# A planner that knows an engine's wait for its own result, finer steps, layer 1 in jobs of 256 tokens, and early room for layer 2's first weights

## The chip, the cores and the metric

The program runs on one core of one Trainium2 chip. The metric is device time in microseconds (us) of one execution, as the median of several. TensorE is called PE here, VectorE DVE, ScalarE ACT, GpSimd POOL, and SyncE, which issues the DMAs, SP.

## What is computed

Three parts run one after the other, all in fp32:

```python
# attention with a complex decay, 4 batches x 8 heads x 768 steps x 48
S_re, S_im = ar*S_re - ai*S_im + k[t] (x) v[t],  ar*S_im + ai*S_re
y[t] = q[t] . S_re                       # 3072 tokens of 384 after the heads are joined
# layer 1, 384 -> 2048 -> 384
x = (relu(x @ w_in) ** 2) @ w_out
# layer 2, the same sizes
h = x @ w2_in;  out = (h * sigmoid(1.702 * h)) @ w2_out
```

## The kernel before

The attention is cut into 12 **units** of 256 tokens, each in two **chunks** of 128. `normalize` scales a unit's decays; `scan` forms their running products: seven steps within groups of 8 (one product L405, then the two planes L408 and L409), five doubling steps across groups (L426 to L429), the exclusive products (L437, L438, into `eexc`) and their use (L448 to L452). It then multiplies q into `tq` (L463) and k into `tk` (L505). Both go through DRAM and come back as `qs`, from which `chunk` computes on PE the scores `pa` (L571), the transposed keys `pk` (L589), the output `px` (L604 to L621), the state `pt` (L641) and its rotation `zs` (L656). Nearly all of the scan is DVE work.

The layers run as **jobs** of tokens (L28). Layer 1 (l=0) has three jobs of 256 tokens, then six of 384; layer 2 (l=1) has eight of 384. A job has 16 **steps** m, one for each 128 of the 2048 inner columns: a first product `h` (L753), ACT's and DVE's work on it (L758 to L768), and a second product into three accumulators (L798, L800). Job 0 multiplies in fp32. From job 1 (first product) and job 3 (second product) on, each fp32 product is made of three with rounded parts (high x high, low x high, high x low), 18 matmuls a step. The rounding of `g` to `gh` is ACT's (L767) and the remainder `gl` DVE's (L768): one `gl` for every step of such a job.

The weights arrive as raw 64-bit words and are decoded by ACT and DVE (L683 to L691, `wf`) and split into a high and a low part (L698, L699). There are 32 such pieces a layer, two a step. All of them live in one ring `w` of 66 buffers, so a piece of layer 2 gets a buffer when one of layer 1 is given back.

The order on all engines is written by a planner (`Plan`, L64) that is run while the program is built. It keeps a list of operations with costs and due times and simulates the engines: it takes the operation that can start first, on a tie the most urgent. What one engine hands to another costs a latency (L69). An operation that needs a result of its own engine could start at once in the plan (L178). What the planner calls one operation stays together: `fin` is two instructions, one doubling step is four (L431). Engines work strictly in the order so made; the waits between them are real semaphores.

Three lines that set the shape of the work:

```python
JOBS = [(0, 256)] * 3 + [(0, 384)] * 6 + [(1, 384)] * 8
...
x.ready = max(x.ready, o.end if x.eng != o.eng else t + o.ns)
...
o = buf("o" if l == 0 else "nt", [128, MX], name="o")
```

Of the kernel before, what the change touches and what calls it, by code (L numbers as in the profile page):

```python
# [24 lines left out]
J = 8  # L25
U = 32 * J
MX = 384
JOBS = [(0, 256)] * 3 + [(0, 384)] * 6 + [(1, 384)] * 8  # L28
NAT1 = 1
# [30 lines left out]
class Op:  # L60
    __slots__ = ("eng", "ns", "lat", "fn", "due", "prio", "pred", "succ", "bufs", "wait", "start", "end", "idx", "ready")


class Plan:  # L64
# [17 lines left out]
    def op(self, eng, ns, fn, r=(), w=(), lat=None, due=1e12):  # L82
        o = Op()
        o.eng, o.ns, o.fn, o.due = eng, float(ns), fn, due
        o.lat = self.LAT[eng] if lat is None else lat
        o.idx, o.succ, o.start = len(self.ops), [], None
        pred = set()
        for k in r:
            if k in self.lastw:
                pred.add(self.lastw[k])  # L90
        for k in w:
# [12 lines left out]
        for x in o.bufs:  # L104
            x.left += 1
        self.ops.append(o)
        return o

    def run(self, issue=None):
# [33 lines left out]
        while len(order) < len(ops):  # L143
# [53 lines left out]
def fast(ctx: ExitStack, tc: tile.TileContext, q, k, v, a_re, a_im, w1, w2, out, flag):  # L197
# [87 lines left out]
    def setup():  # L285
        def consts():
            P.memset(tiny, 2.0 ** -56)
            P.memset(shb, SH * math.log(2.0))
            P.memset(eexc, 0.0)
            P.memset(eexc[:, 0, :, 0:1], 1.0)  # L290

        def more():
            for t in vt + st:
                P.memset(t, 0.0)
            make_identity(nc, ident[:, 0:R])
            P.tensor_copy(ident[:, R:R + D], ident[:, 0:D])
# [4 lines left out]
        op("POOL", 800, consts, w=["consts", "eexc"])  # L301
        op("POOL", 3500, more, w=["v0", "v1", "st0", "st1", "ident", "ones", "tops"], due=30e3)
# [91 lines left out]
    def scan(u):  # L394
# [4 lines left out]
        for j in range(1, J):  # L399
# [6 lines left out]

            def fin(j=j, m=m):
                V.tensor_tensor(ab()[:, 0, j], m()[:, 0, 0], m()[:, 1, 1], ALU.subtract)  # L408
                V.tensor_tensor(ab()[:, 1, j], m()[:, 0, 1], m()[:, 1, 0], ALU.add)  # L409

            js = slice(j, j + 1)
            op("DVE", ve(384), go, r=planes(ab, slice(j - 1, j + 1)), w=[m])
            op("DVE", 2 * ve(96), fin, r=[m], w=planes(ab, js))

        lastp = planes(ab, slice(J - 1, J))
        h = 1
        while h < 32:
            m = buf("mm", [128, 2, 2, 48], name="mm")

            def go(h=h, m=m):  # L420
# [3 lines left out]
                t1, t2 = (m()[:, c].rearrange("p c (n s) -> p c n s", s=h) for c in range(2))  # L424
                lr, li = (gv[:, c, :, 0, h - 1:h].unsqueeze(1).to_broadcast([128, 2, nb, h]) for c in range(2))
                V.tensor_tensor(t1, sec, lr, ALU.mult)  # L426
                V.tensor_tensor(t2, sec, li, ALU.mult)
                V.tensor_tensor(sec[:, 0], t1[:, 0], t2[:, 1], ALU.subtract)
                V.tensor_tensor(sec[:, 1], t1[:, 1], t2[:, 0], ALU.add)  # L429

            op("DVE", 2 * ve(96) + 2 * ve(48), go, r=lastp, w=lastp + [m])  # L431
            h *= 2


        def groups():
            g = ab()[:, :, J - 1].rearrange("p c (x r) -> p c x r", r=32)
            V.tensor_copy(eexc[:, 0:2, :, 1:32], g[:, :, :, 0:31])  # L437
            V.tensor_scalar(eexc[:, 2, :, 1:32], g[:, 1, :, 0:31], -1.0, None, ALU.mult)  # L438

        op("DVE", 310, groups, r=lastp, w=["eexc"])  # L440
        ee = eexc.rearrange("p c x r -> p c (x r)")
        for js in (slice(0, HJ), slice(HJ, J - 1)):
# [6 lines left out]

            op("DVE", ve(192 * n), lambda p2=p2, n=n, mul=mul: mul(p2()[:, :, :n], 1), r=["eexc", *planes(ab, js)], w=[p2])  # L450
            op("DVE", ve(192 * n), lambda js=js, mul=mul: mul(ab()[:, :, js], 0), r=["eexc", *planes(ab, js)], w=planes(ab, js))
# [103 lines left out]
    def chunk(i, due):  # L555
# [115 lines left out]
    def decode(l, m, g):  # L671
# [19 lines left out]
        op("DVE", ve(384), lambda: V.tensor_tensor(w32(), w32(), words()[1], ALU.add), r=[w_, raw, (raw, 0)], w=[w_])  # L691

    def split(l, m, g):

        w_ = wf[l, m, g]
        high = wh[l, m, g] = buf("w", [128, DM], F32R, name="wh")
        low = wl[l, m, g] = buf("w", [128, DM], F32R, name="wl")
        op("ACT", ac(384), lambda: A.copy(high(), w_()), r=[w_], w=[high])  # L698
        op("DVE", ve(384), lambda: V.tensor_tensor(low(), w_(), high().bitcast(F32), ALU.subtract), r=[w_, high], w=[low])  # L699

# [36 lines left out]
    def first_product(j, m, due):  # L737
# [34 lines left out]
    def second_product(j, m, parts, due):  # L772
# [84 lines left out]
    for j, (l, t0, n) in enumerate(jobs):  # L857
# [215 lines left out]
```

## Time and profile before

| | |
|---|---|
| median of 3 runs | 1100.03 us (1096.93 to 1100.8) |
| the profiled execution | 1100.76 us, span 1099.1 us |
| PE busy | 982.4 us (89%), 6994 matmuls |
| DVE busy | 762.6 us (69%) |
| ACT busy | 593.1 us (54%) |
| PE's granted clock, mean | 0.982 |

The span runs from the first to the last instruction of the profiled execution. An engine's busy time counts the durations of its instructions, and two that overlap count once. Matmuls overlap and their ends are modelled, so PE's busy time says less than the distance from one matmul's start to the next. The views read below are the page's chain of waits, the busy time by stage, the timeline of one engine, the groups of instructions by shape, and the waits.

### The profile page before, as it was taken

Reading aid. Unit: us, or ns where it says so; the run is one execution under the profiler, and the core shown is the slowest. Engines: PE = TensorE matmul, PEld = TensorE weight load, DVE = VectorE, ACT = ScalarE, POOL = GpSimd, SP = SyncE. Lnnn points to the kernel's source line nnn. Section 1 sums busy time; section 2 is a strip of 40 time slices with the busy share of each in tenths; the row PEclk is TensorE's granted clock in tenths of the full one; section 3 lists DMA queues with packets and bytes.
Section 4 is the critical chain, followed back from the end, with each engine's and each line's share of the span. In section 5 each row is a group of like instructions: output and inputs, shape, how many; then the busy total and the mean of one; then the engine's idle time right before and its main releaser. Section 6 shows DMA issues by size and latency. Waiting matters only on the chain.

```text
span 1099.1 us, 18699 instructions
## 1 busy us (share of the span) xinstructions
PE 982.4 (89%) x6994; PEld 945.0 (86%) x6994; DVE 762.6 (69%) x1503; ACT 593.1 (54%) x1339; POOL 59.6 (5%) x70
## 2 busy tenths in 40 slices
PE   0058769998999999989999999989999999999997
PEld 0056648987899999989999999989999999999996
DVE  7998899999998989988883268893434343443332
ACT  4536558655666576665755489773434343433332
POOL 1010100100101010120000100000000000000000
PEclk9989889999899999999999999999999999999999
DMA  6468748356654554447543234421101010000000
GB/s 186 115 145 220 175 147 190 65 143 138 127 123 102 138 138 110 110 92 145 131 94 81 59 109 130 144 87 45 40 4 44 1 44 1 22 1 23 1 22 25
DMA packets 132180, 102.14 MB, mean 93 GB/s; under 512 B 46704, under 2 KB 123888, under 8 KB 132080
## 3 DMA queue, kind: packets, MB, share of 16 engines
q1 hardware_dynamic: 132080, 100.85, 37.4%
q8 instruction: 57, 0.93, 0.4%
q14 instruction: 43, 0.35, 0.1%
HBM read 72.43 MB, written 28.39 MB: 92 GB/s over the span
## 4 chain that ended last, share of the span: by engine, by line
PE 56%; DVE 26%; ACT 6%; DMA 5%; issue 4%; SPq 1%; POOL 1%; DVEq 0%
PE h L753 26%; PE acc L800 17%; PE acc L798 8%; DVE mm L405 3%; DMA scr<-tq 2%; DVE tk L505 1%; DVE gl L768 1%; DVE m L448 1%; DVE ab L448 1%; DVE wf L691 1%; DVE ab L346 1%; DVE wf L689 1%; DVE wl L699 1%; PE pa L571 1%; DVE ab L409 1%
## 5 line engine op out<-in xcount | busy, mean ns | idle before, releaser
L768 DVE TENSOR_TENSOR gl<-g,gh 128x384 fp32r<-128x384 f32 x224 | 125.0, 558 | 98.4 <-ACT gh L767 89.1
L753 PE MATMUL h<-xh,wh 128*128 128x384 f32 (+1 forms) x768 | 175.7, 337 | 2.0 <-ACT wh L698 1.0
L762 DVE TENSOR_TENSOR g<-g,h 128x384 f32<-128x384 f32 x128 | 70.8, 553 | 148.7 <-ACT g L761 148.6
L753 PE MATMUL h<-xh,wl 128*128 128x384 f32 (+1 forms) x768 | 172.6, 333 | 0.4 <-DVE wl L699 0.3
L753 PE MATMUL h<-xl,wh 128*128 128x384 f32 (+1 forms) x768 | 171.3, 331 | 1.9 <-DVE xl L633 1.9
L767 ACT CAST gh<-g 128x384 fp32r<-128x384 f32 x224 | 115.0, 513 | 67.9 <-DVE g L762 64.9
L761 ACT ACTIVATE g<-h 128x384 f32<-128x384 f32 x128 | 62.7, 490 | 153.4 <-PE h L753 153.4
L753 PEld LDWEIGHTS h<-xh,wh 128*128 128x128 f32 x768 | 134.9, 189 | 5.3 <-ACT g L758 1.4
L753 PEld LDWEIGHTS h<-xl,wh 128*128 128x128 f32 x768 | 134.4, 188 | 3.2 <-DVE xl L633 2.4
L753 PEld LDWEIGHTS h<-xh,wl 128*128 128x128 f32 x768 | 134.3, 188 | 2.2 <-issue 1.2
L758 ACT ACTIVATE g<-h 128x384 f32<-128x384 f32 (+1 forms) x144 | 64.7, 449 | 109.2 <-PE h L753 101.0
L571 PE MATMUL pa<-qs 96*128 96x128 f32 x384 | 54.0, 295 | 67.8 <-DMA qs<-scr 66.5
L571 PEld LDWEIGHTS pa<-qs 96*128 96x128 f32 x384 | 50.3, 206 | 71.0 <-DMA qs<-scr 61.6
L800 PE MATMUL acc<-wh,gh 128*128 128x384 f32 x384 | 92.2, 335 | 2.0 <-ACT gh L767 2.0
L800 PE MATMUL acc<-wh,gl 128*128 128x384 f32 x384 | 93.2, 338 | 0.4 <-DVE gl L768 0.3
L800 PE MATMUL acc<-wl,gh 128*128 128x384 f32 x384 | 92.5, 336 | 0.0
L575 POOL TENSOR_SCALAR_AFFINE_SELECT asb<-asb 128x512 f32<-128x512 f32 x48 | 56.2, 1179 | 569.7 <-ACT asb L579 569.2
L798 PE MATMUL acc<-g,wf 128*128 128x256 f32 x288 | 70.8, 387 | 3.4 <-ACT g L759 1.8
L759 ACT ACTIVATE g<-g 128x384 f32<-128x384 f32 (+1 forms) x144 | 70.5, 490 | 4.2
L798 PE MATMUL acc<-gl,wh 128*128 128x384 f32 x288 | 71.1, 341 | 1.2 <-DVE gl L768 1.2
L798 PE MATMUL acc<-gh,wh 128*128 128x384 f32 x288 | 70.9, 341 | 0.0
L800 PEld LDWEIGHTS acc<-wh,gh 128*128 128x128 f32 x384 | 68.3, 188 | 2.7 <-ACT gh L767 2.3
(114 smaller groups left out, 1649.0 us busy)
## 6 DMA issues: line engine op xcount, KB each, us to landing
raw<-in_w_dram SPq DMA_DIRECT2D x64, 384.0 KB
scr<-tq SPq DMA_DIRECT2D x24, 384.0 KB
qs<-scr SPq DMA_DIRECT2D x48, 129.0 KB
qs<-scr SPq DMA_DIRECT2D x48, 128.0 KB
scr<-tk SPq DMA_DIRECT2D x12, 390.0 KB
nat_re<-in_a_re_dram SPq DMA_DIRECT2D x48, 96.0 KB
nat_im<-in_a_im_dram SPq DMA_DIRECT2D x48, 96.0 KB
nat_q<-in_q_dram SPq DMA_DIRECT2D x48, 96.0 KB
```

The lines of the kernel that those rows point to most:

```text
L405: V.tensor_tensor(m(), x, y, ALU.mult)
L571: T.matmul(pa()[:, h], lhsT=qs()[:, 4 * g + h, kcol], rhs=qs()[:, 4 * g + h, qcol], start=True, stop=True)
L575: P.affine_select(out=tj, in_=tj, pattern=[[0, 4], [1, J], [J, C // J]], base=0, channel_multiplier=-1, compare_op=ALU.is_ge, fill=0.0)
L753: T.matmul(h()[:, :n], lhsT=ww()[:, kk * 128:kk * 128 + 128], rhs=xx()[:, kk, :n], start=(i == kk == 0), stop=(i == len(terms) - 1 and kk ...
L758: op("ACT", ac(n) - 30, lambda: A.activation(g()[:, :n], h()[:, :n], AF.Relu), r=[h], w=[g])
L759: op("ACT", ac(n), lambda: A.activation(g()[:, :n], g()[:, :n], AF.Square), r=[g], w=[g])
L761: op("ACT", ac(n) - 30, lambda: A.activation(g()[:, :n], h()[:, :n], AF.Sigmoid, scale=1.702), r=[h], w=[g])
L762: op("DVE", ve(n), lambda: V.tensor_tensor(g()[:, :n], g()[:, :n], h()[:, :n], ALU.mult), r=[h, g], w=[g])
L767: op("ACT", ac(n), lambda: A.copy(gh()[:, :n], g()[:, :n]), r=[g], w=[gh])
L768: op("DVE", ve(n), lambda: V.tensor_tensor(gl()[:, :n], g()[:, :n], gh()[:, :n].bitcast(F32), ALU.subtract), r=[g, gh], w=[gl])
L798: T.matmul(acc[i]()[:, :n], lhsT=ww()[:, i * 128:i * 128 + 128], rhs=gg()[:, :n], **st_)
L800: T.matmul(acc[i](), lhsT=gg()[:, i * 128:i * 128 + 128], rhs=ww(), **st_)
```

## The change

It has five parts. The planner gets a table `OWN`: an operation that reads a result of its own engine can start 95 ns after that result's instruction on DVE, ACT and POOL. Operations are cut finer: `fin` into two, a doubling step into four. Layer 1 runs in 12 jobs of 256 tokens. The two `eexc` operations and the first state copy of each batch go from DVE to ACT. Layer 2's weights of steps 0 to 7 (16 of 32 pieces) put their high and low parts into buffers of the attention (`homes`), and their decoding stands in the program one job earlier; layer 2's output copies use the ring `o` of two buffers, not `nt` of four.

```diff
-JOBS = [(0, 256)] * 3 + [(0, 384)] * 6 + [(1, 384)] * 8
+JOBS = [(0, 256)] * 12 + [(1, 384)] * 8
...
+    OWN = {"PE": 0, "DVE": 95, "ACT": 95, "POOL": 95, "SP": 0}
...
-                x.ready = max(x.ready, o.end if x.eng != o.eng else t + o.ns)
-                if o.eng == "SP":
+                if x.eng != o.eng or o.eng == "SP":
                     x.ready = max(x.ready, o.end)
+                else:
+                    x.ready = max(x.ready, t + o.ns + (self.OWN[o.eng] if o.idx in x.raw else 0))
...
-            op("DVE", 2 * ve(96), fin, r=[m], w=planes(ab, js))
+            op("DVE", ve(96), lambda j=j, m=m: V.tensor_tensor(ab()[:, 0, j], m()[:, 0, 0], m()[:, 1, 1], ALU.subtract),
+               r=[m], w=planes(ab, js, (0,)))
+            op("DVE", ve(96), lambda j=j, m=m: V.tensor_tensor(ab()[:, 1, j], m()[:, 0, 1], m()[:, 1, 0], ALU.add),
+               r=[m], w=planes(ab, js, (1,)))
...
-            op("DVE", 2 * ve(96) + 2 * ve(48), go, r=lastp, w=lastp + [m])
+            for c in range(2):
+                op("DVE", ve(96), lambda c=c, times=times: times(c), r=lastp, w=[(m, c)])
+            for c in range(2):
+                op("DVE", ve(48), lambda c=c, both=both: both(c), r=[(m, 0), (m, 1)], w=[lastp[c]])
...
-        op("DVE", 310, groups, r=lastp, w=["eexc"])
+        op("ACT", 240, lambda: A.copy(eexc[:, 0:2, :, 1:32], g()[:, :, :, 0:31]), r=lastp, w=["eexc"])
+        op("ACT", 170, lambda: A.mul(eexc[:, 2, :, 1:32], g()[:, 1, :, 0:31], -1.0), r=[lastp[1]], w=["eexm"])
...
-                op("DVE", ve(384), lambda: V.tensor_copy(heads(s1), pt()), r=[pt], w=[s1k])
+                op("ACT", ac(384), lambda: A.copy(heads(s1), pt()), r=[pt], w=[s1k])
...
+    homes = [("nat", "nat"), ("nat", "qk"), ("nt", "nt"), ("nt", "nt"), ("tq",), ("ab",), ("qs",), ("qs",)]
...
-                o = buf("o" if l == 0 else "nt", [128, MX], name="o")
+                o = buf("o", [128, MX], name="o")
...
-        if l == 0 and j + 1 < nl0:
-            attention(j + 1)
+        if j == nl0 - 1:
+            for m, g in ws[:2 * len(homes)]:
+                decode(1, m, g)
+                split(1, m, g)
+        if j == nl0:
+            for m, g in ws[2 * len(homes):]:
+                decode(1, m, g)
+                split(1, m, g)
```

Three places show what this does to the order. The first is DVE in the scan of a unit, while the weights of layer 1 are split beside it (`mm` is the product of one step, `ab` the running products, `wl` a weight's low part). Before:

```order
L405 TENSOR_TENSOR mm_1582<-ab_805 128x384
L408 TENSOR_TENSOR ab_805<-mm_1582 128x96
L409 TENSOR_TENSOR ab_805<-mm_1582 128x96
L699 TENSOR_TENSOR wl_1593<-wf_1227,wh_1580 128x384
L405 TENSOR_TENSOR mm_1603<-ab_805 128x384
```

And now (L408 is the former L405, L412 and L414 the two planes, L720 the former L699):

```order
L408 TENSOR_TENSOR mm_1631<-ab_888 128x384
L720 TENSOR_TENSOR wl_1634<-wf_255,wh_1624 128x384
L412 TENSOR_TENSOR ab_888<-mm_1631 128x96
L414 TENSOR_TENSOR ab_888<-mm_1631 128x96
L720 TENSOR_TENSOR wl_1647<-wf_284,wh_1636 128x384
L408 TENSOR_TENSOR mm_1654<-ab_888 128x384
```

A second foreign instruction now stands between the product and the two instructions that read it.

The second place is DVE at the last unit's key product, the last large piece of attention work there (`tk`; `nt` and `kt` belong to it, `z` and `st` to a state, `gl` to a step of a layer 1 job). Before:

```order
L768 TENSOR_TENSOR gl<-g,gh 128x384
L497 SCALAR_TENSOR_TENSOR kt<-kt,nt 128x768
L505 TENSOR_TENSOR tk<-kt,ab 128x8x3x32 x2
L768 TENSOR_TENSOR gl<-g,gh 128x384 x5
L633 TENSOR_TENSOR xl<-px,xh 128x3x128
```

And now (L504, L512, L792 are the former L497, L505, L768; `w_7864` is the low part of a weight of layer 2):

```order
L792 TENSOR_TENSOR gl<-g,gh 128x256
L504 SCALAR_TENSOR_TENSOR kt<-kt,nt 128x768
L512 TENSOR_TENSOR tk<-kt,ab 128x8x3x32 x2
L672 TENSOR_TENSOR st_80<-st_80,z 96x8x48
L792 TENSOR_TENSOR gl<-g,gh 128x256 x2
L720 TENSOR_TENSOR w_7864<-wf,w_7774 128x384 x2
L792 TENSOR_TENSOR gl<-g,gh 128x256
```

Of the 96 `gl` of layer 1, 69 stood ahead of this product before; now 117 of 144 do. Both leave 27 steps behind it, of 384 tokens before and of 256 now. The splitting of layer 2's weights begins right behind it.

The third place is ACT where one job of layer 2 ends (`o` is the output's copy out of an accumulator, of which there are three). Before:

```order
L814 COPY o<-acc_8677 128x384
L814 COPY o<-acc_8683 128x384
L767 CAST gh<-g 128x384
L814 COPY o<-acc_8688 128x384
L761 ACTIVATE g<-h 128x384
```

And now:

```order
L838 COPY o<-acc_9939 128x384
L838 COPY o<-acc_9945 128x384
L791 CAST gh<-g 128x384
L785 ACTIVATE g<-h 128x384
L791 CAST gh<-g 128x384
L838 COPY o<-acc_9965 128x384
```

The third copy, which now needs the buffer of the first, has moved behind two more instructions.

## Rows read from the trace of the kernel before

**Rows 1.** The page: the chain that ended last, share of the span by engine
```profile
PE 56%; DVE 26%; ACT 6%; DMA 5%; issue 4%; SPq 1%; POOL 1%; DVEq 0%
```

**Rows 2.** Busy time by stage; the last columns are PE's clock, DMA share, GB/s
```profile
core 0: us, PE busy (x) PEld busy (x) DVE busy (x) ACT busy (x) POOL busy (x), PEclk, DMA share, GB/s
58.00:174.20 116.20, 85.23 (x623) 70.31 (x623) 105.32 (x219) 66.54 (x174) 9.28 (x8) 0.91 0.70 178
174.20:585.40 411.20, 394.96 (x3305) 376.42 (x3306) 377.75 (x741) 262.28 (x579) 41.32 (x34) 0.98 0.53 119
585.40:690.00 104.60, 104.60 (x798) 103.12 (x798) 55.12 (x111) 75.59 (x174) 5.62 (x6) 1.00 0.39 106
690.00:750.00 60.00, 56.56 (x318) 54.44 (x317) 49.34 (x104) 40.02 (x101) 0.00 (x0) 1.00 0.36 114
```

**Rows 3.** Chain of waits in order of time, 585 to 590 us: start, us, what
```profile
585.55 1.79 PE pa L571 x16
...
587.87 1.57 PE h L753 x9
```

**Rows 4.** Timeline of DVE, 55 to 58 us: start, us, instruction
```profile
55.07 0.56 DVE L405 TENSOR_TENSOR mm<-ab 128x384 f32<-128x384 f32 x1
55.67 0.26 DVE L408 TENSOR_TENSOR ab<-mm 128x96 f32<-128x96 f32 x1
55.84 0.25 DVE L409 TENSOR_TENSOR ab<-mm 128x96 f32<-128x96 f32 x1
...
57.21 0.55 DVE L689 SCALAR_TENSOR_TENSOR wf<-raw,wf 128x384 int32<-128x384 int32 x1
57.67 0.55 DVE L405 TENSOR_TENSOR mm<-ab 128x384 f32<-128x384 f32 x1
```

**Rows 5.** Timeline of PE in job 2, three matmuls of 256 columns a row
```profile
219.41 0.52 PE L753 MATMUL h<-xh,wl 128*128 128x256 f32 x3
219.76 0.52 PE L753 MATMUL h<-xl,wh 128*128 128x256 f32 x3
```

**Rows 6.** Timeline of PE at the start of job 3, the first of 384
```profile
273.66 4.09 PE L571 MATMUL pa<-qs 96*128 96x128 f32 x16 [4.31 <-DMA qs<-scr]
277.55 1.16 PE L589 MATMUL pk<-ident,qs 96*128 96x96 f32 x8
...
287.03 0.79 PE L753 MATMUL h<-xl,wh 128*128 128x384 f32 x3 [1.88 <-DVE xl L633]
```

**Rows 7.** Timeline of PE, 484 to 493 us, in a later job of 384
```profile
484.28 1.56 PE L641 MATMUL pt<-v,ktn 128*96 128x48 f32 x16 [1.76 <-ACT ktn L592]
485.68 3.04 PE L571 MATMUL pa<-qs 96*128 96x128 f32 x16
488.37 1.31 PE L798 MATMUL acc<-gl,wh 128*128 128x384 f32 x3
...
492.60 0.43 PE L604 MATMUL px<-asb,v 128*32 128x128 f32 x8 [1.19 <-POOL asb L575]
```

**Rows 8.** Groups by shape: busy us, mean ns, then idle before and its releaser
```profile
L758 ACT ACTIVATE g<-h 128x256 f32<-128x256 f32 x48 | 18.1, 377 | 29.8 <-PE h L753 29.8
L759 ACT ACTIVATE g<-g 128x256 f32<-128x256 f32 x48 | 20.0, 417 | 1.3
L767 ACT CAST gh<-g 128x384 fp32r<-128x384 f32 x224 | 115.0, 513 | 67.9 <-DVE g L762 64.9
L768 DVE TENSOR_TENSOR gl<-g,gh 128x384 fp32r<-128x384 f32 x224 | 125.0, 558 | 98.4 <-ACT gh L767 89.1 <-PE acc L798 6.7 <-ACT asb L579 1.4
L437 DVE COPY eexc<-ab 128x186 f32<-128x186 f32 x12 | 3.6, 299 | 0.4
```

**Rows 9.** Waits of PE, 690 to 760 us: us in total, times, longest
```profile
PE acc L800 <- ACT gh L767: 2.0, 1, 2.0
PE h L753 <- ACT wh L698: 1.0, 1, 1.0
```

**Rows 10.** Timeline of SP at the end: the three output DMAs of the last job
```profile
1090.56 2.00 SPq L815 DMA_DIRECT2D out_dram<-o  x3
```

More of the change, by code (lines that the diff above doesn't have):

```diff
@@ L60 @@
 class Op:
-    __slots__ = ("eng", "ns", "lat", "fn", "due", "prio", "pred", "succ", "bufs", "wait", "start", "end", "idx", "ready")
+    __slots__ = ("eng", "ns", "lat", "fn", "due", "prio", "pred", "raw", "succ", "bufs", "wait", "start", "end", "idx", "ready")
 class Plan:
     LAT = {"PE": 260, "DVE": 160, "ACT": 170, "POOL": 160, "SP": 0}
+    OWN = {"PE": 0, "DVE": 95, "ACT": 95, "POOL": 95, "SP": 0}
     def __init__(self):
@@ L86, in op @@
         o.idx, o.succ, o.start = len(self.ops), [], None
-        pred = set()
+        pred, o.raw = set(), set()
         for k in r:
@@ L90, in op @@
                 pred.add(self.lastw[k])
+                o.raw.add(self.lastw[k])
         for k in w:
@@ L299, in more @@
                 P.memset(tops[:, c:c + n], top)
-        op("POOL", 800, consts, w=["consts", "eexc"])
+        op("POOL", 800, consts, w=["consts", "eexc", "eexm"])
         op("POOL", 3500, more, w=["v0", "v1", "st0", "st1", "ident", "ones", "tops"], due=30e3)
@@ L418, in scan, with parts @@
             m = buf("mm", [128, 2, 2, 48], name="mm")
-            def go(h=h, m=m):
+            def parts(h=h, m=m):
                 nb = 96 // (2 * h)
@@ L423, in go, with times, both @@
                 sec = gv[:, :, :, 1, :]
[L424 to L429, printed above, removed]
-            op("DVE", 2 * ve(96) + 2 * ve(48), go, r=lastp, w=lastp + [m])
-            h *= 2
[L435 to L438, printed above, removed]
-        op("DVE", 310, groups, r=lastp, w=["eexc"])
+                t = [m()[:, c].rearrange("p c (n s) -> p c n s", s=h) for c in range(2)]
+                left = [gv[:, c, :, 0, h - 1:h].unsqueeze(1).to_broadcast([128, 2, nb, h]) for c in range(2)]
+                return sec, t, left
+            def times(c, parts=parts):
+                sec, t, left = parts()
+                V.tensor_tensor(t[c], sec, left[c], ALU.mult)
+            def both(c, parts=parts):
+                sec, t, _ = parts()
+                V.tensor_tensor(sec[:, c], t[0][:, c], t[1][:, 1 - c], (ALU.subtract, ALU.add)[c])
+            for c in range(2):
+                op("DVE", ve(96), lambda c=c, times=times: times(c), r=lastp, w=[(m, c)])
+            for c in range(2):
+                op("DVE", ve(48), lambda c=c, both=both: both(c), r=[(m, 0), (m, 1)], w=[lastp[c]])
+            h *= 2
+        g = lambda: ab()[:, :, J - 1].rearrange("p c (x r) -> p c x r", r=32)
+        op("ACT", 240, lambda: A.copy(eexc[:, 0:2, :, 1:32], g()[:, :, :, 0:31]), r=lastp, w=["eexc"])
+        op("ACT", 170, lambda: A.mul(eexc[:, 2, :, 1:32], g()[:, 1, :, 0:31], -1.0), r=[lastp[1]], w=["eexm"])
         ee = eexc.rearrange("p c x r -> p c (x r)")
@@ L448, in mul @@
                 V.tensor_tensor(o, ab()[:, :, js], e, ALU.mult)
-            op("DVE", ve(192 * n), lambda p2=p2, n=n, mul=mul: mul(p2()[:, :, :n], 1), r=["eexc", *planes(ab, js)], w=[p2])
+            op("DVE", ve(192 * n), lambda p2=p2, n=n, mul=mul: mul(p2()[:, :, :n], 1), r=["eexc", "eexm", *planes(ab, js)], w=[p2])
             op("DVE", ve(192 * n), lambda js=js, mul=mul: mul(ab()[:, :, js], 0), r=["eexc", *planes(ab, js)], w=planes(ab, js))
@@ L691, in decode @@
         op("DVE", ve(384), lambda: V.tensor_tensor(w32(), w32(), words()[1], ALU.add), r=[w_, raw, (raw, 0)], w=[w_])
+    homes = [("nat", "nat"), ("nat", "qk"), ("nt", "nt"), ("nt", "nt"), ("tq",), ("ab",), ("qs",), ("qs",)]
     def split(l, m, g):
         w_ = wf[l, m, g]
[L696 to L699, printed above, removed]
+        if l == 1 and m < len(homes):
+            if g == 0:
+                rings = homes[m]
+                n = 2 if len(rings) == 2 else 4
+                made = [buf(r, [128, n, DM], F32R, name="w2") for r in rings]
+                home[m] = [(made[0], 0), (made[-1], n - 2)]
+            (hb, h0), (lb, l0) = home[m]
+            high, low = (lambda: hb()[:, h0 + g], (hb, h0 + g)), (lambda: lb()[:, l0 + g], (lb, l0 + g))
+        else:
+            hb, lb = buf("w", [128, DM], F32R, name="wh"), buf("w", [128, DM], F32R, name="wl")
+            high, low = (hb, hb), (lb, lb)
+        wh[l, m, g], wl[l, m, g] = high, low
+        op("ACT", ac(384), lambda: A.copy(high[0](), w_()), r=[w_], w=[high[1]])
+        op("DVE", ve(384), lambda: V.tensor_tensor(low[0](), w_(), high[0]().bitcast(F32), ALU.subtract),
+           r=[w_, high[1]], w=[low[1]])
+    home = {}
     jobs, nxt = [], [0, 0]
@@ L783, in second_product @@
             high, low = wh[l, m, 1], wl[l, m, 1]
-            terms = ((high, gh, [high]), (low, gh, [low]), (high, gl, [high]))
+            terms = ((high[0], gh, [high[1]]), (low[0], gh, [low[1]]), (high[0], gl, [high[1]]))
         nr = KT if l == 0 else n // 128
@@ L863, in fast @@
                 split(0, m, 1)
-        if j == nl0:
-            for m, g in ws:
+        if l == 0 and j + 1 < nl0:
+            attention(j + 1)
+        if j == nl0 - 1:
+            for m, g in ws[:2 * len(homes)]:
                 decode(1, m, g)
                 split(1, m, g)
-        if l == 0 and j + 1 < nl0:
-            attention(j + 1)
+        if j == nl0:
+            for m, g in ws[2 * len(homes):]:
+                decode(1, m, g)
+                split(1, m, g)
         if l == 1:
```

5 lines of the change are left out of this document (1 added, 4 removed).

## The prediction

> **What bounds the kernel now.** I read the chain of waits first: PE holds 56% of it and DVE 26% [rows 1]. So two engines bound this kernel, and the question is where each does. Busy time by stage answers it [rows 2]. The stages are cut at the end of the third unit's key product (174.2 us), of the last unit's (585.4 us), and at the passage into layer 2. From 58 to 174.2 us DVE is busy 105.32 of 116.20 us, PE 85.23, at a granted clock of 0.91 (a mean over its two levels, 2.4 and 1.2 GHz): PE starves behind DVE, which scans and decodes weights. From 174.2 to 585.4 us DVE is busy 377.75 and PE 394.96 of 411.20 us at a clock of 0.98: both are nearly full and each waits for the other at times. From 585.4 us on DVE has half of its time free, and PE is busy 104.60 of 104.60 us. Only the passage into layer 2 loses a little: 56.56 of 60 us from 690 to 750. Behind 585.4 us the reader should see nothing but PE in the chain, back to back: nine split matmuls of 384 columns take 1.57 us, 0.174 each [rows 3].
>
> So nothing done to DVE or ACT behind 585.4 us can pay, apart from the passage. What can be gained lies in front of it: PE idles since its tokens are late, and that time is never made up.
>
> **Part 1, the wait for an engine's own result.** The timeline of DVE shows its price. A 384-element product whose result is read next holds DVE from 55.07 to 55.67 us, 0.60 us; L689, which also handles 384 elements and which the next instruction does not read, holds it for 57.67 - 57.21 = 0.46 us. Between instructions without such a wait the starts lie closer than a duration: L409 follows L408 after 0.17 us though L408 lasts 0.26 [rows 4]. A wait avoided is thus worth 0.60 - 0.46 = 0.14 us at most; I take 0.12, since the short operations have less to lose.
>
> By the order, an instruction that reads the result of the one just ahead of it stood on DVE 114 times before the third unit's key product; now 40. Up to the last one it was 341 and is 217. The first stage follows DVE, so there the 74 waits go straight into the time: 74 x 0.12 = 9 us earlier. Of the remaining 50 fewer (6 us), DVE gives back as much: it does three more decodings and 117 `gl` in place of 69 before the last key product, so behind 174.2 us I expect no shorter DVE work, only more of PE's work fed by it.
>
> The Trainium skill, VectorE: DVE Perf Modes, section The DRAIN you can't avoid, says the opposite of these rows: the next operation does not start before the pipe is empty, and a semaphore after each operation costs nothing extra. By that rule these 9 us would be zero. The rows disagree: 0.17 us between starts at a duration of 0.26, and 0.60 against 0.46.
>
> The operations sent to ACT (L437 and its sibling, 12 times each, 0.30 us a piece [rows 8], and four state copies) I put at zero. DVE loses some 7 us of work, but by the order its next instruction in four of twelve units waits at once for ACT's answer, and the others have one to three instructions between. If ACT is late by 1 us in each unit this costs 12 us; if never, it gains 7.
>
> **Part 2, jobs of 256.** PE does 2592 split matmuls of 256 columns for 1728 of 384. The fed interval at 256 is 0.353 us for three [rows 5], 0.1177 each, against 0.174 x 2/3 = 0.116: 2592 x 0.1177 - 1728 x 0.1744 = +3.7 us on PE's path. The fp32 work of jobs 0 to 2 stays. `gl` costs DVE about 5 us more through its fixed share, ACT's three passes some 27 us of busy time: ACT has 262.28 of 411.20 us busy [rows 2], so there is cover.
>
> What it brings is where a job may start. A job of 384 needs one and a half units, one of 256 exactly one. Job 3's start shows the price: PE idles 4.31 us for `qs`, takes 277.55 - 273.66 = 3.89 us for scores that take 1.79 when fed [rows 3, 6], and idles 1.88 us more for `xl`: 8.3 us. A second hole at 484 to 493 us holds 1.76 + 1.19 us of idle time and 0.9 us of slow scores [rows 7]: 3.9 us. These 12.2 us are the sure part. The whole that is visible in this stage is 411.20 - 394.96 = 16.2 us idle and 2% of 411 us lost to the lower clock, 8.2 us: 24.4 us. I take the middle, **18 us**.
>
> The order asks for more. 27 steps stand behind the last key product in both programs, of 18 x 0.1744 = 3.14 us before and 18 x 0.1177 = 2.12 now, so 27.6 us of PE work has moved ahead of it. That exceeds the 24.4 us that are visibly free, so I don't take it whole; it is the lower end.
>
> **Part 3, layer 2's early weights.** By the order 21 of 32 pieces are decoded when layer 2's first gate product is due on DVE, before it was 16. The cover is the third stage: DVE is busy 55.12 and ACT 75.59 of 104.60 us, five more pieces cost each some 10. What it removes are PE's waits of 2.0 and 1.0 us in the passage [rows 9] and the slow restarts behind them: **-3 us** of the 60 - 56.56 that are idle there. If the cover were gone, PE would wait here for `wh` as before, so between 0 and -3.4.
>
> **Part 4, two output buffers.** The third copy of a job waits for the first one's DMA. Within layer 2 the order has put a first product of 9 matmuls (1.57 us) ahead of its accumulator's next use and two ACT instructions ahead of the copy, so I put it at zero. At the very end nothing hides it: the first output DMA is issued at 1090.56 us, all three within 2.00 us [rows 10], and the span ends at 1099.1. The third copy and its issue now wait for the first landing. Between 0 and the 8.5 us that the whole tail lasts I take **+2 us**, as a landing that began 1.4 us before the third issue lags it by little. SP issues nine more stores of layer 1, hidden in its queue's slack.
>
> **Sum.** Against the profiled execution's own 1100.8 us (0.7 above the median): -9 (first stage) - 18 (mixed stage) - 3 (passage) + 3.7 (matmul rate) + 2 (tail) = -24.3, so **1076.5 us**, forecast 1077. Bounds: -12 to 0 for the first stage with the ACT transfer, -27.6 to 0 for the mixed stage.
>
> **Rivals.**
> - *The order's whole count comes true.* PE keeps pace and 27.6 us in place of 18 leave the tail: 1067, with less lost at the lower clock down to 1058. For it: the plan gives every unit one job exactly. Against: 30 us more of PE's work must pass in a stage that is already 96% busy (394.96 of 411.20). Chance 0.22.
> - *Waits for own results cost what any neighbour costs.* Then the first stage gains nothing: 1077 + 9 = 1086. 0.60 against 0.46 us [rows 4] speaks against it; for it, a late `eexc` answer of ACT would eat the same 9 us. Chance 0.12. The rule of the Trainium skill (VectorE: DVE Perf Modes, The DRAIN you can't avoid) would lead here.
> - *The holes move.* Every job now begins at a unit's end, so PE meets a fresh dependency twelve times in place of nine, and the mixed stage gains nothing: 1095. Against it: by the order a unit's key product stands a full job ahead of the job that uses it. Chance 0.10.
> - *Slower: the step becomes too short for its chain.* A step of 256 gives PE 2.12 us; `h` must pass ACT (377 and 417 ns), ACT again and DVE (513 and 558 at 384, so some 400 each at 256) [rows 8], about 1.6 us and four hand-overs, on an ACT that also serves the scan. Two `h` buffers cover two steps, which should do. If ACT's queue stretches it so that PE stalls in each of the 144 steps, the gain of 24 us is gone at 0.17 us a step, and at 0.3 us a step the time is 1077 + 43 = 1120. Chance 0.06.
> - That the change does not do what it says is seen partly in the order: only five more pieces come early, and 217 waits remain. The sum has that in it.
>
> **How the numbers follow.** The forecast has 0.50. The range runs from 1057 (the whole count, less clock loss) to 1096 (the holes move): it leaves out the slow case and the tails, some 0.15. A measurement here tells 0.5%, 5.5 us, from no change. Faster than 1094.5: 0.50 + 0.22 + 0.12 and a share of the moved holes, 0.86. Same 0.08, slower 0.06.
>
> **What would show it.** In the new trace the third key product should end near 165 us, the last one between 575 and 590 us. PE's granted clock up to there should rise above 0.91 and 0.98. PE should stand in the chain alone from about the last key product on, with some 57 us of layer 1 left in steps of 2.12 us; the passage should lack the 2.0 us wait. Idle PE ahead of `h` or `acc` in most steps, released by ACT, would mean the slow rival. A first stage that still ends at 174 us, with a mixed stage shorter, would refute the price of the own wait; holes of several us at each job's start would refute part 2.

## The result and the profile after

The changed kernel takes 1071.18 us (median of 4; 1070.51 to 1072.91) against 1099.78 us: a ratio of 0.9746, 95% interval 0.9725 to 0.9768. Its profiled execution has a span of 1071.1 us, 28.0 us less than the 1099.1 us before.

The page's chain of waits, by engine, answers to [rows 1]:

```profile
PE 79%; DVE 7%; DMA 5%; ACT 4%; issue 2%; SPq 1%; POOL 1%; DVEq 0%; ACTq 0%
```

PE's share rose from 56% to 79%, DVE's fell from 26% to 7%. The busy time by stage is cut at the ends of the third and the last key product on DVE and at the start of layer 1's last matmul on PE (PE, PEld, DVE, ACT, POOL busy, then granted clock, DMA share, GB/s). [rows 2] come close: their 174.2 us is the end of the first of the third product's two instructions, the second ends at 175.6 us.

```profile
66.00:168.90 102.90, 90.05 (x640) 76.17 (x641) 91.59 (x194) 65.55 (x171) 7.44 (x8) 0.95 0.70 177
168.90:591.80 422.90, 418.05 (x4270) 402.16 (x4269) 386.17 (x779) 295.95 (x768) 41.33 (x36) 1.00 0.53 118
591.80:656.60 64.80, 64.80 (x660) 64.13 (x660) 47.16 (x104) 57.04 (x159) 3.85 (x4) 1.00 0.55 160
656.60:720.00 63.40, 60.56 (x345) 59.45 (x344) 45.07 (x94) 39.50 (x96) 0.00 (x0) 1.00 0.29 91
```

In the mixed stage PE is now busy 418.05 of 422.90 us at a clock of 1.00, before 394.96 of 411.20 at 0.98. The timelines of DVE give the two key products, first of the kernel before, then of the changed one (start, duration):

```profile
172.58 3.03 DVE L505 TENSOR_TENSOR tk<-kt,ab 128x768 f32<-128x768 f32 x2
582.15 3.27 DVE L505 TENSOR_TENSOR tk<-kt,ab 128x768 f32<-128x768 f32 x2
```

```profile
165.94 3.00 DVE L512 TENSOR_TENSOR tk<-kt,ab 128x768 f32<-128x768 f32 x2 [0.30 <-DMA scr<-tq]
588.66 3.14 DVE L512 TENSOR_TENSOR tk<-kt,ab 128x768 f32<-128x768 f32 x2
```

The third ends 6.7 us earlier (175.6 to 168.9), the last 6.4 us later (585.4 to 591.8). But layer 1's last matmul starts 64.8 us behind the last one, before it was 101.4: PE has done far more by then. The first unit is later: its key product ends at 54.0 us in place of 50.4, and PE's first matmul comes 4.4 us later. The waits of PE in the mixed stage, between those two products, show that the holes of [rows 6, 7] are gone (us in total, times, longest; no wait for `qs` or `ktn` is left):

```profile
PE h L777 <- ACT g L782: 1.5, 3, 0.8
PE px L611 <- POOL asb L582: 1.1, 3, 0.5
PE acc L822 <- DVE gl L792: 0.7, 2, 0.6
```

Behind the passage into layer 2, from 656 to 800 us, against [rows 9]:

```profile
PE h L777 <- DVE g L786: 1.5, 2, 0.9
PE acc L824 <- ACT o L834: 1.4, 1, 1.4
```

At the end PE's last matmul is over at 1060.5 us and the span at 1071.1: 10.6 us, before 8.0. The timelines of ACT and SP show the third copy waiting for the first one's DMA, against [rows 10]:

```profile
1063.95 0.48 ACT L838 COPY o<-acc 128x384 f32<-128x384 f32 x1 [3.42 <-DMA out_dram<-o]
```

```profile
1060.73 4.33 SPq L839 DMA_DIRECT2D out_dram<-o  x2
```

To compare kernels I take from each stage the work that PE did in it: every matmul record at its fed distance from start to start (0.1743 us for a split matmul of 384 columns, 0.1175 of 256, 0.2155 for each of the two records of an fp32 one; 0.111 scores, 0.082 transposes, 0.0825 states, 0.0275 outputs, 0.325 rotations). What is left of the stage is PE's **lost time**. The whole work is 945.4 us before and 948.8 after. The first stage is counted from PE's first matmul; "layer 2" runs from layer 1's last matmul to the last one of all. The third stage, from the last key product to layer 1's end, loses 1.2 us before and nothing after; it has no column.

The 0.1175 was read in the kernel before and is a little too long. In the changed kernel's third stage, where PE never idles, 459 distances behind a split matmul of 256 columns have a mean of 0.115 us; three a row, 0.34 us from row to row:

```profile
650.04 0.50 PE L777 MATMUL h<-xh,wh 128*128 128x256 f32 x3
650.38 0.50 PE L777 MATMUL h<-xh,wl 128*128 128x256 f32 x3
650.72 0.50 PE L777 MATMUL h<-xl,wh 128*128 128x256 f32 x3
```

By 0.115 the whole work is 944.7 us before and 941.6 after, and the mixed stage loses 33.9 us before and 17.0 after. Every kernel with layer 1 in jobs of 256 then loses 5 to 6 us more in the mixed stage than the table says, e2 and e8 half a us.

Each ratio is to runs of the kernel before on the same chip: e1 to e8 ran on one where it takes 1103 to 1104 us, e9 to e12 on another, at 1100.7. The other columns come from one profile each. Six of the kernels (the change, e2, e4, e5, e7, e8) give DVE the same order up to the third key product, and it ends between 167.0 and 171.2 us; e5 has the change's order up to the last one as well and ends that 5.2 us later. A few us in these columns thus tell nothing.

| kernel | ratio to before, interval | third, last key product | lost: first | mixed | layer 2 | tail |
|---|---|---|---|---|---|---|
| before | 1 | 175.6, 585.4 | 43.8 | 33.3 | 5.7 | 8.0 |
| the change | 0.9746 (0.9725 to 0.9768) | 168.9, 591.8 | 30.4 | 11.1 | 4.8 | 10.6 |
| e1 jobs alone | 1.0225 (1.0200 to 1.0251) | 177.7, 592.8 | 45.6 | 38.3 | 25.5 | 8.0 |
| e2 old jobs | 0.9940 (0.9919 to 0.9961) | 167.2, 588.4 | 29.8 | 41.6 | 1.4 | 10.6 |
| e3 table at zero | 0.9874 (0.9853 to 0.9895) | 177.4, 600.1 | 40.8 | 21.8 | 5.3 | 10.6 |
| e4 late weights | 0.9883 (0.9859 to 0.9908) | 167.4, 591.3 | 28.4 | 13.7 | 26.8 | 8.0 |
| e5 third buffer | 0.9706 (0.9684 to 0.9728) | 171.2, 597.0 | 31.9 | 14.0 | 2.3 | 8.4 |
| e6 eexc on DVE | 0.9723 (0.9700 to 0.9747) | 169.9, 592.4 | 21.7 | 17.1 | 2.8 | 10.8 |
| e7 half units | 1.0081 (1.0050 to 1.0111) | 168.8, 606.2 | 29.2 | 22.3 | 1.2 | 10.8 |
| e8 table, steps, ACT | 0.9975 (0.9956 to 0.9994) | 167.0, 588.6 | 27.5 | 46.0 | 4.9 | 8.4 |
| e9 jobs and weights | 1.0094 (1.0060 to 1.0128) | 175.1, 595.9 | 43.7 | 35.3 | 5.4 | 10.6 |
| e10 coarse steps | 0.9666 (0.9635 to 0.9696) | 161.1, 571.5 | 25.9 | 6.4 | 2.2 | 10.1 |
| e11 e5 and e6 | 0.9680 (0.9656 to 0.9704) | 169.2, 589.9 | 22.9 | 15.4 | 1.1 | 8.1 |
| e12 e11, table at 190 | 0.9726 (0.9692 to 0.9760) | 169.9, 593.1 | 26.2 | 12.1 | 1.2 | 8.6 |

### The profile page after: what moved, and what is told of

The parts are those of the page before. It is cut to its first block, busy times and chain, and to the rows that moved or that the text cites. A ratio compares the mean times of both kernels' runs of the same rounds, so it can differ in the third digit from the quotient of the medians.

```text
span 1071.1 us, 20775 instructions
## 1 busy us (share of the span) xinstructions
PE 974.0 (91%) x7858; PEld 941.8 (88%) x7858; DVE 753.4 (70%) x1523; ACT 610.9 (57%) x1520; POOL 56.0 (5%) x70
## 3 DMA queue, kind: packets, MB, share of 16 engines
q1 hardware_dynamic: 133376, 100.85, 38.3%
## 4 chain that ended last, share of the span: by engine, by line
PE 79%; DVE 7%; DMA 5%; ACT 4%; issue 2%; SPq 1%; POOL 1%; DVEq 0%; ACTq 0%
PE h L777 33%; PE acc L824 19%; PE acc L822 16%; PE pa L578 4%; PE pt L648 2%; DMA x2d<-o 1%; DMA raw<-in_w_dram 1%; PE px L611 1%; PE pk L596 1%; PE px L623 1%; POOL asb L582 1%; PE px L628 1%; DVE m L455 1%; PE px L617 1%; DVE ab L455 1%
## 5 line engine op out<-in xcount | busy, mean ns | idle before, releaser
L792 DVE TENSOR_TENSOR gl<-g,gh 128x256 fp32r<-128x256 f32 (+1 forms) x272 | 133.0, 491 | 85.6 <-ACT gh L791 64.9
L791 ACT CAST gh<-g 128x256 fp32r<-128x256 f32 (+1 forms) x272 | 124.1, 459 | 80.4 <-DVE g L786 77.4
L777 PE MATMUL h<-xh,wh 128*128 128x256 f32 (+1 forms) x720 | 140.3, 303 | 3.5 <-ACT g L782 2.6
L777 PE MATMUL h<-xh,wl 128*128 128x256 f32 (+1 forms) x720 | 133.8, 294 | 0.9 <-DVE wl L720 0.9
L777 PE MATMUL h<-xl,wh 128*128 128x256 f32 (+1 forms) x720 | 133.8, 294 | 0.0
L582 POOL TENSOR_SCALAR_AFFINE_SELECT asb<-asb 128x512 f32<-128x512 f32 x48 | 52.6, 1103 | 560.1 <-ACT asb L586 559.7
L783 ACT ACTIVATE g<-g 128x256 f32<-128x256 f32 x192 | 79.9, 421 | 3.5
L822 PE MATMUL acc<-gl,wh 128*128 128x256 f32 x432 | 80.8, 282 | 0.9 <-DVE gl L792 0.7
L824 PE MATMUL acc<-w,gh 128*128 128x384 f32 x384 | 79.9, 337 | 1.4 <-ACT o L834 1.4
L822 PE MATMUL acc<-gh,wh 128*128 128x256 f32 x432 | 80.5, 281 | 0.0
L822 PE MATMUL acc<-gh,wl 128*128 128x256 f32 x432 | 80.0, 280 | 0.0
```

Of the source, the lines that this page charges most:

```text
L582: P.affine_select(out=tj, in_=tj, pattern=[[0, 4], [1, J], [J, C // J]], base=0, channel_multiplier=-1, compare_op=ALU.is_ge, fill=0.0)
L777: T.matmul(h()[:, :n], lhsT=ww()[:, kk * 128:kk * 128 + 128], rhs=xx()[:, kk, :n], start=(i == kk == 0), stop=(i == len(terms) - 1 and kk ...
L783: op("ACT", ac(n), lambda: A.activation(g()[:, :n], g()[:, :n], AF.Square), r=[g], w=[g])
L791: op("ACT", ac(n), lambda: A.copy(gh()[:, :n], g()[:, :n]), r=[g], w=[gh])
L792: op("DVE", ve(n), lambda: V.tensor_tensor(gl()[:, :n], g()[:, :n], gh()[:, :n].bitcast(F32), ALU.subtract), r=[g, gh], w=[gl])
L822: T.matmul(acc[i]()[:, :n], lhsT=ww()[:, i * 128:i * 128 + 128], rhs=gg()[:, :n], **st_)
```

## The experiments

**e1, the jobs alone** (the kernel before with one line changed):

```diff
-JOBS = [(0, 256)] * 3 + [(0, 384)] * 6 + [(1, 384)] * 8
+JOBS = [(0, 256)] * 12 + [(1, 384)] * 8
```

> The kernel before with one line changed: layer 1 in 12 jobs of 256. Theory A (the mixed stage is shortened by where jobs begin, the first stage by the avoided own waits): third key product still near 175 us, about 18 us less PE time lost up to the last key product, 3.4 us more matmul time: 1084 us. Theory B (the order of DVE does it all; shorter jobs alone only move the holes): by its order 40 steps of 2.12 us stand behind the last key product, 85 us as in the kernel before, so the time stays at 1098 to 1103 us.

1130.61 us, ratio 1.0225: 25 us slower, outside both expectations. The mixed stage loses 38.3 us in place of 33.3, so shorter jobs alone win nothing there. They shorten PE's wait for `qs`, as part 2 of the prediction has it, but PE then waits longer for DVE's `xl` and `gl`. Its waits in the mixed stage, in the kernel before and then in e1:

```profile
PE pa L571 <- DMA qs<-scr: 4.3, 1, 4.3
PE acc L798 <- DVE gl L768: 1.2, 2, 0.7
PE pa L571 <- DVE xl L633: 1.2, 1, 1.2
```

```profile
PE pa L571 <- DVE xl L633: 6.0, 4, 3.1
PE acc L798 <- DVE gl L768: 4.7, 7, 1.5
PE pa L571 <- DMA qs<-scr: 1.0, 1, 1.0
```

The large new loss is where neither theory looked, behind the passage into layer 2. PE's waits there, 697 to 800 us, and the stage's busy time:

```profile
PE acc L800 <- ACT gh L767: 9.1, 5, 2.0
PE h L753 <- DVE g L762: 2.4, 2, 1.7
```

```profile
697.30:760.00 62.70, 50.58 (x237) 45.98 (x235) 48.99 (x100) 41.36 (x104) 0.00 (x0) 0.89 0.39 126
```

PE is busy 50.58 of 62.70 us, with the clock down to 0.89 (a mean of 1.2 and 2.4 GHz), while DVE decodes: 18 pieces' worth in this stretch. By the order 11 pieces of layer 2 are decoded ahead of its first gate product, before it was 16. A last job of 256 is over sooner than one of 384, so fewer buffers of the ring `w` may have come free early; no run shows that apart. The loss follows the count of pieces: about 26 us with 11 (e1, e4), 5 to 6 with 15 or 16 (before, e8), 1 to 5 with 20 or more.

**e2, the old jobs in the changed kernel** (e1's line the other way round).

> The changed kernel with the old list of jobs (three of 256, six of 384). Theory A: the first stage keeps its gain (third key product at 169 us), the mixed stage loses its own and has its holes at job starts again: 1100 - 8 + 2 for the end = 1092 to 1094 us. Theory B: most of the gain is kept, 1072 to 1080 us. By the order 26 steps of 3.14 us stand behind the last key product, 3 us less than before, and 102 own waits are gone (11 us): 1086 us by that count.

Ratio 0.9940: theory A's size, 7 us faster than before in place of 28. The first stage keeps its gain (167.2), the mixed one loses 41.6 us, 8.3 more than before. Most of those 8.3 is one hole, that of [rows 6], grown from 4.31 to 11.68 us; PE's waits for `qs` in this stage add up to 17.5 us:

```profile
274.69 4.22 PE L578 MATMUL pa<-qs 96*128 96x128 f32 x16 [11.68 <-DMA qs<-scr]
```

**e3, the planner's table at zero.**

```diff
-    OWN = {"PE": 0, "DVE": 95, "ACT": 95, "POOL": 95, "SP": 0}
+    OWN = {"PE": 0, "DVE": 0, "ACT": 0, "POOL": 0, "SP": 0}
```

> The changed kernel with the table OWN set to zero, so that the planner again lets an operation read a result of its own engine at once; steps stay cut finer, jobs stay at 256. 319 instructions of DVE directly behind the one whose result they read up to the last key product, in place of 217, 109 in place of 40 up to the third. Theory A: third key product back to 175 to 177 us, the mixed stage as in the changed kernel: 1079 us. If the order's count of steps left (32 in place of 27) comes on top: 1086 to 1089. If an own wait costs nothing, as the DRAIN rule has it: 1071 us.

Ratio 0.9874, the upper expectation. The third key product ends at 177.4 us:

```profile
174.37 3.06 DVE L512 TENSOR_TENSOR tk<-kt,ab 128x768 f32<-128x768 f32 x2 [0.53 <-DMA scr<-tq]
```

69 more own waits (109 against 40) cost 177.4 - 168.9 = 8.5 us, 0.12 us each, as the prediction priced them; against the 167.0 to 171.2 us of the six kernels it is 0.09 to 0.15. The price can also be read within one kernel, with no change of order. In the changed kernel the product L408 is followed 40 times by an instruction that does not read it, 0.469 us from start to start (median), and 42 times by L412, which does, 0.593 us. One of each:

```profile
60.22 0.54 DVE L408 TENSOR_TENSOR mm<-ab 128x384 f32<-128x384 f32 x1
60.69 0.54 DVE L698 CUSTOM_DVE_ANT_0 wf<-raw,wf 128x768 uint16<-128x768 uint16 x1
...
67.07 0.56 DVE L408 TENSOR_TENSOR mm<-ab 128x384 f32<-128x384 f32 x1
67.66 0.26 DVE L412 TENSOR_TENSOR ab<-mm 128x96 f32<-128x96 f32 x1
```

The mixed stage loses 21.8 us in place of 11.1. In all the table is worth 1.3%, 14 us. The Trainium skill, VectorE: DVE Perf Modes, section The DRAIN you can't avoid, says that the next operation waits for the pipe to empty and that a semaphore after each operation costs nothing extra, but also that a next operation that is not held starts earlier. The 0.593 against 0.469 us go against the second of these and agree with the third.

**e4, layer 2's weights late, output buffers as before.**

```diff
-    homes = [("nat", "nat"), ("nat", "qk"), ("nt", "nt"), ("nt", "nt"), ("tq",), ("ab",), ("qs",), ("qs",)]
+    homes = []
...
-                o = buf("o", [128, MX], name="o")
+                o = buf("o" if l == 0 else "nt", [128, MX], name="o")
```

> The changed kernel with layer 2's weights as in the kernel before: no buffers of the attention for them, decoding at the first job of layer 2, and the ring of four for layer 2's output copies. 11 pieces decoded before layer 2's first gate product in place of 20. Theory A (PE does not miss those pieces, and the two output buffers cost the end 2.6 us): 1068 to 1072 us. Rival (the early room is what makes the passage smooth, DVE and ACT can't decode 21 pieces while layer 2 runs): PE waits of 5 to 15 us behind the passage, 1074 to 1085 us.

Ratio 0.9883, the rival's side: 15 us over the change. The loss lies behind the passage, 26.8 us in place of 4.8, while the tail is back at 8.0. PE's waits of 657 to 800 us:

```profile
PE acc L824 <- ACT gh L791: 11.9, 7, 1.9
PE acc L824 <- ACT o L834: 1.2, 1, 1.2
```

The waits are within the rival's 5 to 15 us. Together with e1: jobs of 256 lose some 20 us at layer 2's start, and the early room takes them back. With the old jobs the same room is worth 4 us only (e8 to e2).

**e5, a third output buffer.**

```diff
-                o = buf("o", [128, MX], name="o")
+                o = buf("mm" if i == 2 and (l == 1 or t0 + n == NT) else "o", [128, MX], name="o")
```

> The changed kernel; the third output copy of every job of layer 2, and of layer 1's last job, takes the buffer of the scan's products (free by then) in place of the first copy's. If the two buffers cost what the trace of the changed kernel shows (2.6 us longer tail behind the last matmul, 1.4 us of PE's wait for the copy in the passage): 3 to 4 us less than the changed kernel, ratio to the kernel before 0.971. If the tail is only DMA time and the wait is covered by another behind it: no change, 0.9746.

Ratio 0.9706, as expected. The tail is 8.4 us, layer 2 loses 2.3 us, and the three DMAs are issued in a row again:

```profile
1064.70 2.01 SPq L839 DMA_DIRECT2D out_dram<-o  x3
```

**e6, the operations on eexc and the first state copies back on DVE.**

```diff
-        op("ACT", 240, lambda: A.copy(eexc[:, 0:2, :, 1:32], g()[:, :, :, 0:31]), r=lastp, w=["eexc"])
+        op("DVE", 200, lambda: V.tensor_copy(eexc[:, 0:2, :, 1:32], g()[:, :, :, 0:31]), r=lastp, w=["eexc"])
...
-                op("ACT", ac(384), lambda: A.copy(heads(s1), pt()), r=[pt], w=[s1k])
+                op("DVE", ve(384), lambda: V.tensor_copy(heads(s1), pt()), r=[pt], w=[s1k])
```

> The changed kernel with the two operations on eexc and the first state copies back on DVE. Theory A (their move is worth nothing: DVE loses 7 us of work and waits for ACT as long): 1071 us, ratio 0.974 to 0.977. Rival (DVE sets the first stage and ACT answers in time): third key product 1 to 2 us later, last one 5 to 7 us later, ratio 0.979 to 0.981.

Ratio 0.9723 (0.9700 to 0.9747), theory A's side. It overlaps the change's interval: the move can't be told from nothing.

**e7, boundaries in mid-unit.**

```diff
-JOBS = [(0, 256)] * 12 + [(1, 384)] * 8
+JOBS = [(0, 256)] * 3 + [(0, 128)] + [(0, 256)] * 8 + [(0, 128)] + [(1, 384)] * 8
```

> The changed kernel with the boundaries of layer 1's jobs 3 to 11 moved by half a unit: three jobs of 256, one of 128, eight of 256, one of 128. Two jobs of 128 replace one of 256, which costs PE some 10 us if a matmul of 128 columns takes as long as loading its weights. Theory A1 (what counts is that a job begins where a unit ends): PE loses 30 us or more in the mixed stage, a wait for qs at the job starts, as with the old list of jobs. Theory A2 (what counts is the shorter job, wherever it begins): PE loses 11 to 16 us there as in the changed kernel.

1112.65 us, ratio 1.0081, some 37 us over the change. Most of that is the matmul itself. Three split matmuls of 128 columns a row, in the last job:

```profile
690.31 0.50 PE L822 MATMUL acc<-gh,wh 128*128 128x128 f32 x3
690.64 0.50 PE L822 MATMUL acc<-gh,wl 128*128 128x128 f32 x3
690.98 0.50 PE L822 MATMUL acc<-gl,wh 128*128 128x128 f32 x3
```

0.335 us for three, 0.1115 each, nearly what 256 columns take: two jobs of 128 cost 576 x (0.1115 - 0.1175 / 2) = 30 us more than one of 256, not some 10. With those at 0.1115 the mixed stage loses 22.3 us, between the two expectations: no hole of A1's size, no wait for `qs`, but 11 us more than the change. Where a job begins may count; the two jobs of 128 disturb this run too much to say.

**e8, table, steps and moves to ACT, with old jobs and late weights** (e2's and e4's edits together).

> The changed kernel with the old list of jobs and with layer 2's weights and output buffers as before: what is left is the planner's table, the finer steps and the operations moved to ACT. If parts just add up: the first stage gains 8 us, the mixed one loses 8 as with the old jobs and early weights, the passage is as before (5.7 us lost), the tail too: 1100 us, ratio 0.997 to 1.000. If the early room for weights is worth 15 us with these jobs too: ratio 1.005 to 1.01.

Ratio 0.9975 (0.9956 to 0.9994): as the sum of parts. What the first stage wins (its key product ends 8.6 us earlier) the mixed one loses (46.0 against 33.3).

**e9, jobs and early weights alone** (e1, and from the change the early decoding with its buffers and the output copies in `o`).

> The kernel before with two parts of the change: layer 1 in 12 jobs of 256, and the early room for layer 2's weights with the shared output buffers. No table OWN, no finer steps, nothing moved to ACT. Theory C (the early weights remove the 20 us that the shorter jobs alone lost at the start of layer 2; the planner's knowledge and the finer steps decide how many steps stand ahead of the last key product): passage 5 us lost in place of 25, tail 10.6, mixed stage as with the jobs alone (38 us lost), 36 steps behind the last key product by the order: ratio 1.000 to 1.008. Rival (weights and jobs together are the whole change): ratio 0.98 to 0.985.

1111.05 us, ratio 1.0094 (1.0060 to 1.0128), theory C's side. The passage is cured (5.4 us lost for e1's 25.5), the mixed stage is not (35.3). Weights and jobs are not the whole change; without the planner's part they are a loss.

**e10, coarse steps** (`fin` as one operation of two instructions, a doubling step as one of four, the rest of the change kept):

```diff
-            op("DVE", ve(96), lambda j=j, m=m: V.tensor_tensor(ab()[:, 0, j], m()[:, 0, 0], m()[:, 1, 1], ALU.subtract),
-               r=[m], w=planes(ab, js, (0,)))
-            op("DVE", ve(96), lambda j=j, m=m: V.tensor_tensor(ab()[:, 1, j], m()[:, 0, 1], m()[:, 1, 0], ALU.add),
-               r=[m], w=planes(ab, js, (1,)))
+            op("DVE", 2 * ve(96), fin, r=[m], w=planes(ab, js))
...
-            for c in range(2):
-                op("DVE", ve(96), lambda c=c, times=times: times(c), r=lastp, w=[(m, c)])
-            for c in range(2):
-                op("DVE", ve(48), lambda c=c, both=both: both(c), r=[(m, 0), (m, 1)], w=[lastp[c]])
+            op("DVE", 2 * ve(96) + 2 * ve(48), go, r=lastp, w=lastp + [m])
```

> The changed kernel with the scan's steps as coarse as before (two and four instructions to one operation); the table OWN, the jobs of 256, the moves to ACT and the early weights stay. By the order 40 own waits up to the third key product and 210 up to the last, as in the changed kernel, but 32 steps in place of 27 behind the last. If the steps' count decides: 10 us more, ratio 0.983 to 0.986. If the waits decide: 1071 us, ratio 0.973 to 0.977.

1063.64 us, ratio 0.9666: faster than the change, outside both expectations. The order's 32 steps behind the last key product are there (layer 1 ends 75 us behind it, for 65), but that product itself ends at 571.5 us, 20 us earlier:

```profile
157.96 3.09 DVE L505 TENSOR_TENSOR tk<-kt,ab 128x768 f32<-128x768 f32 x2
568.35 3.19 DVE L505 TENSOR_TENSOR tk<-kt,ab 128x768 f32<-128x768 f32 x2 [0.44 <-DVE kt L497]
```

The two profiles exaggerate: e10's is the fastest of its four executions and the change's the slowest of its own, 13.0 us apart where the medians are 7.5. But 161.1 and 571.5 us lie outside what kernels with the change's order show, and with 40 own waits up to the third product in both, their number alone does not set that time. Up to the last product DVE is busy 527.98 of 571.50 us, in the change 534.54 of 591.80: of the 20 us nearly 14 are idle time. Part of it are DVE's waits for ACT, in the change and then here (the same three places; us, times, longest):

```profile
DVE xl L640 <- ACT xh L637: 6.8, 5, 3.8
DVE m L455 <- ACT eexc L447: 6.3, 7, 2.3
DVE nt L383 <- ACT nt L379: 4.8, 5, 1.3
```

```profile
DVE m L448 <- ACT eexc L440: 4.4, 8, 0.9
DVE nt L383 <- ACT nt L379: 1.3, 2, 1.1
DVE xl L633 <- ACT xh L630: 0.6, 2, 0.4
```

These three shrink from 17.9 to 6.3 us. So beside the table the finer steps cost 0.8%, some 9 us. Why the finer order meets ACT late more often was not separated. Without the table it is the other way round: from e9 to e3 the finer steps and the moves to ACT come in, and the ratio falls from 1.0094 to 0.9874, 24 us. And from e9 to e10 the table and the moves come in, with coarse steps: 1.0094 to 0.9666, 47 us. If the moves are worth as little there as in e6, the table is worth far more with coarse steps than the 14 us of e3, and finer steps are a poorer substitute for it.

**e11, e5 and e6 together, and e12, the same with the table at 190 ns.**

> The changed kernel with the third output copy in a buffer of its own and the eexc operations and first state copies back on DVE: both edits by themselves gave 0.9706 and 0.9723. If they add up: 0.968 to 0.971. If the second was only chance: 0.9706.

> As the run before, with the table OWN at 190 ns in place of 95 for DVE, ACT and POOL. 28 own waits up to the third key product in place of 41, 213 in place of 225 up to the last, 26 steps in place of 27 behind it. If the gain came from the planner's table being right about the chip (an avoided wait is worth 0.12 us): 1 to 2 us less in the first stage and 2 us at the end, ratio 0.967 to 0.970. If 95 is where the chip is and more only delays work that could go: same or up to 5 us more.

0.9680 (0.9656 to 0.9704) and 0.9726 (0.9692 to 0.9760). The first is within what was expected, though it can't be told from e5; the second gains nothing, so a table of 190 ns buys nothing here. e10 and e11 are the two fastest kernels that ran. Coarse steps with a third output buffer were not tried.

## Why the prediction was right

The forecast was 1077 us, the time is 1071.18, inside the range. By its own steps, with a split matmul of 256 columns at the measured 0.115 us where nothing else is said:

1. **First stage, -9.** PE's lost time from the span's start to the third key product fell by 9 us (105.6 to 96.7); the product ends 6.7 us earlier. e3 and the two distances of L408 confirm cause and price, about 0.12 us an own wait.
2. **Mixed stage, -18.** Lost time fell by 17 us (33.9 to 17.0; 22.2 by the table). The size is right, the reason given is half of it. The prediction put it down to where jobs of 256 may start and called 12.2 us "the sure part". Such jobs do remove the waits for `qs`: 4.3 us before, 1.0 in e1 and e9, none in the change, but 17.5 and 20.5 with the old jobs (e2, e8). Alone they win nothing, since PE then waits for DVE: e1 and e9 lose no less than the kernel before. That is the rival "the holes move", given 0.10, and the planner's part takes these holes away. The planner's part with the old jobs loses as well (e2, e8). The failed step is that part 2 was costed alone. With the jobs and the early weights the mixed stage loses, by the columns above, 35.3 us with neither the planner's table nor finer steps (e9), 21.8 with finer steps (e3), 11.1 with both (the change) and 6.4 with the table (e10); the last three have the moves to ACT too. That the jobs give the planner places for PE's steps, and that the table lets it put them where DVE really is, fits all of these and is not shown by itself.
3. **The order's count.** The 27 steps behind the last key product came true. Layer 1 takes 64.8 us more from there, before 101.4; the forecast's 57 us left out 9 us of attention work. So did the reason not to take the count whole come true: PE was full, and the mixed stage became 422.9 us long in place of 409.8.
4. **Passage, -3.** It fell by 1 us (5.7 to 4.8). The waits of [rows 9] went, and PE now waits 1.4 us for `o` (L834) and 1.5 us for `g`. The step failed in its bound, "between 0 and -3.4": e4 shows the early weights worth 22 us there. The prediction costed them on the kernel before and missed that jobs of 256 open a loss of 20 us at this place. The sum held since the two errors cancel, which is luck. It also took 21 pieces for decoded early; by the order 20 are.
5. **Matmul rate +3.7, tail +2.** The first has the wrong sign. 0.1177 us was read in job 2 of the kernel before; at 0.115 in the changed kernel the work is 3.1 us less. This term is off by 6.8 us; the whole forecast, for the profiled execution, by 3.6 (1076.5 against 1072.91). The tail is 2.6 us longer. The two output buffers cost 4 us in all (e5), not 2: about half of it is layer 2's (4.8 to 2.3 us lost).
6. **Moves to ACT, 0.** Borne out by e6, within its interval. **Finer steps** had no price of their own beyond the own waits; beside the table they cost 9 us (e10).

Together with 0.8 us in the third stage these give -8.9 - 16.9 - 0.8 - 0.8 - 3.1 + 2.6 = -27.9 us, against 28.0 between the two profiles.

Of its signs, PE's clock rose to 0.95 and 1.00. The 165 us for the third key product were counted from the end of its first instruction (174.2), which is now at 167.5. The last one, at 591.8, is later than the 575 to 590 it gave.

Of the rivals, the slow one did not come: PE's waits for ACT's `g` in the mixed stage are 1.5 us. A slower kernel did lie nearby, at a ratio of 1.0225, but by the jobs' end at layer 2 (e1), a mechanism that the prediction did not name.

## What to carry to other kernels

A planner that does not know an engine's wait for its own result spreads work for a faster machine than it has; one constant of 95 ns was worth 14 us here, and with the old jobs the planner's whole part was worth 3 (e8). The constant by itself, in the kernel before, was not tried. Cost a part of a change on top of the others and not only on the kernel before: shorter jobs alone lost 25 us, and in the changed kernel they gain 21 (e2). Test each part of a winning change by undoing it: one of the five, the finer steps, was a loss beside the table; without it they and the moves to ACT were a gain.

## What the runs showed of the hardware

A DVE instruction that reads the result of the one just ahead of it starts about 0.12 us later than one that does not: 0.593 against 0.469 us behind a product of 384 elements (the changed kernel). One unrelated instruction between the two avoids it: from L698 to an L412 behind it, with L408 ahead of both, it is 0.469 us.

A split matmul's distance from start to start hardly falls below 256 columns: 0.1743 us at 384, 0.115 at 256 (the changed kernel), 0.1115 at 128 (e7), so 256 was the shortest job that costs PE nothing. The Trainium skill, TensorE: Matmul & The Clock Gate, section LDWEIGHTS (loading the stationary operand), lets loading weights take the number of columns over 1.2 GHz, an estimate of 107 ns for 128. The 0.1115 us agree with it as the floor, though no run here took the loads away, and the loads' own records, which overlap, last 0.188 us each.
